# One block for the first batch's product with v, and the steps that stand beside it

## The chip, the cores and the metric

The kernel runs on one core of one Trainium2 chip. The metric is the device time of one execution in microseconds (us); a smaller number is better. The engines are named as in the profile: PE (TensorE), ACT (ScalarE), DVE (VectorE), POOL (GpSimd) and SP (which issues DMAs). A granted clock of 1.00 in the profile is PE's upper level, 2.4 GHz.

## The reference

Two batches of eight heads of attention, with 768 positions of 64 numbers each. A position may look only at positions of its own hash bucket; the bucket is the signs of six projections. The 16 heads' outputs are then the rows of x for a mixture of four experts of two layers each.

```python
q_bits = (np.einsum('bhsd,dk->bhsk', q, proj) > 0)   # 6 bits, the same for k
mask = q_bucket[:, :, :, None] == k_bucket[:, :, None, :]
scores = np.where(mask, scale * np.matmul(q, k.transpose(0, 1, 3, 2)), -1e9)
attn = np.exp(scores - scores.max(-1, keepdims=True)); attn /= attn.sum(-1, keepdims=True) + 1e-09
attn_out = np.matmul(attn, v)                        # batch 2, heads 8, seq 768, head_dim 64
out += p[:, e:e+1] * (np.maximum(x @ w1[e], 0.0) @ w2[e])   # for each of 4 experts
```

## The kernel before

The program has two stages. In the first, the attention of the first batch runs alone, apart from the splitting of the first expert's weights. In the second, the experts' products for the first batch fill PE, and the second batch's attention is woven into them. The edits of this case move work in the first stage only.

`attention()` walks through steps i. Step i is tile t = i mod 6 (128 queries) of head x = i div 6. In each step it calls stages in the order of the letters in `ORDER`, and each engine executes what it was given in the order in which it was given. Each stage works on an older tile or head, by a lag:

- S, scores: four matmuls (L448, L450) into a `sps` tile of PSUM (two tiles in turn), and on DVE a minimum over the row (L455) that also empties `sps`. The second pair of matmuls reads the bucket code in `k2` and `al`.
- E, exponential, lag 1: one ACT instruction (L471).
- T, turning, lag 3: six PE transposes (L516) in two halves, each into a bank of the pool `one` (four banks). A half is emptied by a copy on ACT (L522) or DVE (L520): of three tiles, the first has one copy on each, the second two on ACT, the third one on each. In what follows T0 to T5 are named by the step in which they stand: T3 turns tile 0 of the head, T0 turns tile 3 of the head before.
- V, product with v: twelve column-tiled pairs of matmul records a head (L566) into `pv`, one bank of `one`. `LAG_V` says in which steps after the head's last tile; in the first batch in two parts of six pairs, in steps 3 and 5 of the next head.
- U (L591, L593): `pv` copied out by ACT and DVE, which frees its bank.
- M (L604, L606, L609): three POOL instructions for each half of a pair of heads, in steps 3 and 4 of heads 3, 5 and 7.
- P: the next head's preparation, a generator that goes on by one piece a step. Its pieces are hi (ACT L377 and three POOL copies L265), lo (DVE L380 and one POOL copy), and hash: two pairs of matmuls (L392), their signs by ACT (L402, a pair), and two POOL instructions (L407 and L265) that write the bucket code into `al` and `k2`. The next head's S0 cannot end before that code is there. P also starts the loads of q and k for the head after, and turns them on DVE (L335, here "the turn"), which waits for the hash, since the turned tile takes the place of the one that the hash reads.

Every `W_STEP` pieces of work that `attention()` yields, one piece of the splitting of the first expert's weights is put in (DVE L756, POOL L746).

Of the kernel before, what the change touches and what calls it, by code (L numbers as in the profile page):

```python
# [19 lines left out]
ATT_PACE = 1.52  # L20
LAG_E = 1
SPLIT_AT = (1, 0)
HASH_AT = (3, 0)
LAG_N = (3, 4)
LAG_R = ((6, 4), (7, 6))
LAG_T = 3
LAG_X = 2
LAG_Y = 4
LAG_V = ((4, 6), (7,))
LAST_V = (4, 5)  # L30
LAG_U = (3, 1)
LAG_M = (10, 10)
PP_BUFS = 6
TW = 3
# [9 lines left out]
W_STEP = 6  # L44
PREP_AT = 0
ORDER = "TXSUVMEYNRP"
LIGHT_FROM = 8
DRAIN = 2000
SPLIT_FIRST = 3
FAST = 4  # L50
ALONE = 16
# [5 lines left out]
def tile_lsh_attention__then__domain_moe(  # L57
# [12 lines left out]
    B, H, S, D = q.shape  # L70
    NB = proj.shape[1]
    E, DM, F = w1.shape
    NT = S // P
# [149 lines left out]
    def in_blocks(b, h):  # L223
        return b * H + h in BLOCKS
# [112 lines left out]
    def prep_head(b, h):  # L337
# [27 lines left out]
        else:  # L365
# [4 lines left out]
            steps.setdefault(SPLIT_AT[late] + 1, []).append("lo")  # L370
            steps.setdefault(HASH_AT[late], []).append("hash")
            for at in range(max(steps) + 1):
# [47 lines left out]
    for j in range(KD):  # L420
        t = xp.tile([P, 2, S], F32R, tag=f"x{j}", name="xs0")
# [15 lines left out]
    def mixed(b, h):  # L437
        return b * H + h < LIGHT_FROM

    def heavy(b, h, t):  # L440
        return mixed(b, h)
# [34 lines left out]
    def stage_n(b, h, t):  # L476
        r, o, n = span_of(b, h, t)
        if o != n - 1:
            return
        den = dens.pop((b, h, r))  # L480
        rd = sm.tile([P, NT], F32, tag="rd", name="rd", bufs=2)
        nc.vector.tensor_scalar(out=den[:, :n], in0=den[:, :n], scalar1=1e-9, scalar2=None, op0=ALU.add)
        nc.vector.reciprocal(out=rd[:, :n], in_=den[:, :n])
        rows[b, h, r] = dr.tile([P, n], F32, tag=f"row{n}", name="row", bufs=6)
        nc.sync.dma_start(out=rows[b, h, r], in_=rd[:, :n])

    def stage_r(b, h, t):
        r, o, n = span_of(b, h, t)
        j, odd = divmod(h, 2)
        if t != NT - 1 and (o != n - 1 or not odd):  # L490
            return
        if not odd:
            rdbs[b, j] = xs.tile([P, S], F32, tag="rdb", name="rdb", bufs=1)
        for i in range(r + 1) if not odd else (r,):
            row = rows.pop((b, h, i))
            nc.sync.dma_start(
                out=rdbs[b, j][odd * D : (odd + 1) * D, i * n * P : (i + 1) * n * P],
                in_=row.rearrange("p t -> (p t)").partition_broadcast(D),
            )
# [3 lines left out]
    def stage_t(b, h, t):  # L503
        pt, _ = probs_t.pop((b, h, t))
        g, o = divmod(t, G)
        if o == 0:
            if b or g == 0:
                t0 = pt_tile([P, NT, GN], "pt")
                parts[b, h, g] = [t0[:, a : a + TW] for a in range(0, NT, TW)]
            else:  # L510
                parts[b, h, g] = [hp.tile([P, TW, GN], F32, tag=tag, name="pth") for tag in ("hh", "hl")]
            pts[b, h, g] = [x[:, c] for x in parts[b, h, g] for c in range(TW)]
        for i, a in enumerate(range(0, NT, TW)):
            ps = one("ptps")
            for c in range(TW):
                nc.tensor.transpose(ps[:, c * P : (c + 1) * P], pt[:, (a + c) * P : (a + c + 1) * P], ident)  # L516
            src = ps[:, : TW * P].rearrange("p (c n) -> p c n", c=TW)
            dst = parts[b, h, g][i][:, :, o * P : (o + 1) * P]
            if i and o % 2 == 0:
                nc.vector.tensor_copy(dst, src)  # L520
            else:
                nc.scalar.activation(dst, src, ACTF.Copy)  # L522
# [24 lines left out]
    def stage_y(b, h, g):  # L547
        scr = scrs.pop((b, h, g))
        pt = pt_tile([P, NT, GN], "pt")
        px = pt.rearrange("p c n -> p (c n)")  # L550
        nc.sync.dma_start(out=px.rearrange("p (q x) -> p q x", q=QD), in_=scr.rearrange("q p x -> p q x"))
        px = px.rearrange("p (a c q) -> p c a q", c=NT, q=32)
        pts[b, h, g] = [px[:, c] for c in range(NT)]
# [61 lines left out]
    hseq = [(b, h) for b in range(B) for h in range(H)]  # L615
# [4 lines left out]
    def v_lags(b, h):  # L620
        return LAST_V if (b, h) == (0, H - 1) else LAG_V[not mixed(b, h)]

    def u_lag(b, h):
        return v_lags(b, h)[-1] + (1 if (b, h) == (0, H - 1) else LAG_U[not mixed(b, h)])

# [3 lines left out]
    def attention():  # L629
        n = len(seq)  # L630
        prep = [iter(())]

        def do(op, i):
            if op == "N":
                for b in range(B):
                    j = i - LAG_N[b]
                    if 0 <= j < n and seq[j][0] == b:
                        stage_n(*seq[j])
            elif op == "R":
                for b in range(B):  # L640
                    for odd in range(2):
                        j = i - LAG_R[b][odd]
                        if 0 <= j < n and (seq[j][0], seq[j][1] % 2) == (b, odd):
                            stage_r(*seq[j])
            elif op == "T":
                j = i - LAG_T
                if 0 <= j < n and heavy(*seq[j]):
                    stage_t(*seq[j])
                    return 654
            elif op == "X":  # L650
                j = i - LAG_X
                if 0 <= j < n and not heavy(*seq[j]):
                    stage_x(*seq[j])
            elif op == "Y":
                j = i - LAG_Y
                if 0 <= j < n and j % G == G - 1 and not heavy(*seq[j]):
                    b, h, t = seq[j]
                    stage_y(b, h, t // G)
            elif op == "S":
                if i < n:  # L660
                    b, h, t = seq[i]
                    if t == 0:
                        x = hseq.index((b, h))
                        prep[0] = prep_head(*hseq[x + 1]) if x + 1 < len(hseq) else iter(())
                    stage_s(b, h, t)
                    return 652 + 4270 // NT
                return DRAIN
            elif op == "V":
                for bh, lag in ended(i):
                    for part, at in enumerate(v_lags(*bh)):  # L670
                        if lag == at:
                            stage_v(*bh, part, len(v_lags(*bh)))
                            if (bh, part) == ((0, H - 1), len(v_lags(*bh)) - 1):
                                ready[0] = True
                                return 0
            elif op == "U":
                for bh, lag in ended(i):
                    if lag == u_lag(*bh):
                        stage_u(*bh)
            elif op == "M":  # L680
                for (b, h), lag in ended(i):
                    for g in range(NT // G):
                        if h % 2 and lag == (u_lag(b, h) if (b, h) == (0, H - 1) else LAG_M[b] + g):
                            stage_m(b, h, g)
                if done_b[0] and ready[0]:
                    ready[0] = False
                    return 0
            elif op == "E":
                j = i - LAG_E
                if 0 <= j < n:  # L690
                    stage_e(*seq[j])
            elif op == "P":
                if i < n:
                    b, h, t = seq[i]
                    x = hseq.index((b, h))
                    c = next(prep[0], None) if t >= PREP_AT and x < ALONE else None
                    if t == NT - 1 and x + 2 < len(hseq) and in_blocks(*hseq[x + 2]) and x < ALONE:
                        turn_blocks(*hseq[x + 2])
                    if t == QK_AT and x + 2 < len(hseq):
                        load_qk(*hseq[x + 2])  # L700
                    if t == V_AT and x:
                        load_v(*hseq[x])
                    return c
            return None

        for i in range(n + LAG_M[1] + 3):
            for op in ORDER:
                c = do(op, i)
                if c is not None:
                    yield c  # L710
            x, t = divmod(i, NT)
            if t == NT - 1 and ALONE <= x < len(hseq) - 1:
                for c in prep[0]:
                    yield c
                if x + 2 < len(hseq):
                    turn_blocks(*hseq[x + 2])
                yield ALONE_GAP
# [430 lines left out]
    with tc.manual_schedule():  # L1148
# [6 lines left out]
        i = 0  # L1155
# [21 lines left out]
        for b in range(B):  # L1177
            dm = da = 0.0
            for c in moe(b):
                dm += c  # L1180
                while da < dm * ATT_PACE * n_att / n_moe:
                    x = next(att, None)
# [34 lines left out]
```

## Time and profile before

| | |
|---|---|
| time, median of 3 runs | 706.07 us (705.58 to 706.62) |
| the profiled execution's own time | 705.74 us |
| its span, first to last instruction | 704.0 us |
| PE busy, share of the span | 99% |
| DVE, ACT, POOL busy | 73%, 47%, 44% |
| granted clock of PE | 1.00 throughout |

The profiled execution took 1.7 us more than its span, and it lies 0.33 us under the median of the three runs. A share of busy time is a mean over both stages. PE's matmuls overlap in the profile, so that its busy share hides short waits; the distance from one start to the next tells more.

### The profile page before, as it was taken

The page shows a single profiled execution, that of the slowest core. Times are in us where ns is not written, and L with a number is a line of the kernel's source. Part 1 is how long each engine was busy: PE and PEld are TensorE (multiplying, and loading weights), DVE is VectorE, ACT ScalarE, POOL GpSimd, SP SyncE. Part 2 cuts the span into 40 slices and gives each one's busy share as a digit, 9 for nine tenths or more (in the row PEclk, how much of TensorE's full clock was granted, in tenths as well). Part 3 has the DMA queues.
Part 4 walks back from the last instruction along what each step waited for, and adds up shares of the span by engine and source line. Part 5 has one row for each costly group of instructions (what it writes and reads, how often), then busy time and mean ns, then how long its engine had stood idle before and what let it go on. Part 6 is the DMA issues. An engine that isn't in the chain of part 4 may idle for free.

```text
span 704.0 us, 10120 instructions
## 1 busy us (share of the span) xinstructions
PE 695.8 (99%) x3702; PEld 589.8 (84%) x3702; DVE 513.7 (73%) x840; ACT 330.1 (47%) x645; POOL 307.2 (44%) x290
## 2 busy tenths in 40 slices
PE   8999999999999999999999999999999999999998
PEld 6766676878878878878998989899898989989896
DVE  6898888967668568774767886776767667776862
ACT  6887788544543553551424444243333424343330
POOL 6359578623443543461525555342324324232420
PEclk9999999999999999999999999999999999999999
DMA  5323344759879878683111212421122121122202
GB/s 139 64 52 76 87 104 80 232 168 302 246 223 285 236 251 301 212 284 139 60 63 59 89 63 77 150 71 61 61 89 88 45 78 61 61 60 90 82 9 89
DMA packets 83938, 87.77 MB, mean 125 GB/s; under 512 B 52400, under 2 KB 54960, under 8 KB 81840
## 3 DMA queue, kind: packets, MB, share of 16 engines
q1 hardware_dynamic: 82864, 86.79, 41.1%
q8 instruction: 29, 0.48, 0.3%
q10 hardware_dynamic: 1024, 0.33, 0.2%
q14 instruction: 21, 0.17, 0.1%
HBM read 65.04 MB, written 22.07 MB: 124 GB/s over the span
## 4 chain that ended last, share of the span: by engine, by line
PE 92%; DVE 3%; issue 2%; POOL 2%; ACT 1%; DMA 0%; ACTq 0%; POOLq 0%; DVEq 0%
PE mps L787 12%; PE mps L789 12%; PE mps L788 12%; PE mps L1070 8%; PE mps L1074 8%; PE mps L1073 8%; PE pv L566 8%; PE sps L448 4%; PE sps L450 4%; PE ptps L516 4%; PE mps L837 3%; PE mps L839 3%; PE mps L838 3%; PE hps L392 1%; DVE p L455 1%
## 5 line engine op out<-in xcount | busy, mean ns | idle before, releaser
L787 PE MATMUL mps<-w2hi,hh 128*128 128x512 f32 (+1 forms) x388 | 150.6, 388 | 0.0
L789 PE MATMUL mps<-w2hi,hl 128*128 128x512 f32 (+1 forms) x388 | 150.3, 387 | 0.0
L788 PE MATMUL mps<-w2lo,hh 128*128 128x512 f32 (+1 forms) x388 | 150.3, 387 | 0.0
L1056 POOL TENSOR_TENSOR w2lo<-ws,w2hi 128x512 fp32r<-128x512 f32 x48 | 61.2, 1297 | 150.6 <-ACT w2hi L1055 149.1
L455 DVE TENSOR_SCALAR_CACHE_REDUCE p<-sps 128x768 f32<-128x768 f32 x96 | 90.3, 941 | 26.5 <-PE sps L450 24.9
L471 ACT ACTIVATE p<-p,nb 128x768 f32<-128x768 f32 x96 | 89.5, 932 | 25.3 <-DVE p L455 24.9
L781 DVE SCALAR_TENSOR_TENSOR acc<-mps,pe,acc 128x512 f32<-128x512 f32 (+1 forms) x85 | 63.0, 742 | 49.5 <-PE mps L789 48.8
L1074 PE MATMUL mps<-xo,w1lo 128*128 128x384 f32 x272 | 91.4, 336 | 0.0
L1070 PE MATMUL mps<-xo,w1hi 128*128 128x384 f32 x272 | 91.3, 336 | 0.0
L1073 PE MATMUL mps<-xo,w1hi 128*128 128x384 f32 x272 | 91.3, 336 | 0.0
L1080 ACT ACTIVATE hh<-mps 128x384 fp32r<-128x384 f32 x96 | 47.3, 493 | 92.5 <-PE mps L1074 62.9
L789 PEld LDWEIGHTS mps<-w2hi,hl 128*128 128x128 f32 x388 | 72.9, 188 | 15.3
L787 PEld LDWEIGHTS mps<-w2hi,hh 128*128 128x128 f32 x388 | 72.9, 188 | 14.5 <-issue 0.6
L788 PEld LDWEIGHTS mps<-w2lo,hh 128*128 128x128 f32 x388 | 72.9, 188 | 14.0
L1100 DVE TENSOR_TENSOR mt<-mps,mt 128x384 f32<-128x384 f32 x72 | 40.2, 558 | 44.5 <-PE mps L1074 43.7
L1014 POOL TENSOR_TENSOR w1lo<-ws,w1hi 128x512 fp32r<-128x512 f32 x36 | 49.4, 1377 | 43.8 <-ACT w1hi L1010 16.5
L566 PE MATMUL pv<-pt,tv 128*64 128x384 f32 x288 | 67.2, 492 | 0.0
L1085 DVE SCALAR_TENSOR_TENSOR hl<-mps,hh 128x384 fp32r<-128x384 f32 x96 | 53.4, 556 | 15.4 <-ACT hh L1080 13.1
L1010 ACT ACTIVATE w1hi<-wc 128x512 fp32r<-128x512 f32 x48 | 30.0, 630 | 69.8 <-DVE wc L1019 69.8
L265 POOL TENSOR_SCALAR q<-ah 64x768 fp32r<-64x768 f32 (+1 forms) x33 | 27.1, 823 | 77.3 <-ACT ah L377 63.0
L448 PE MATMUL sps<-ah,q 128*128 128x384 f32 x192 | 54.1, 363 | 1.3 <-DVE p L455 1.3
L535 DVE STREAM_TRANSPOSE t<-p 128x768 f32<-128x768 f32 x48 | 46.2, 963 | 9.3 <-ACT p L471 9.1
(136 smaller groups left out, 1368.8 us busy)
## 6 DMA issues: line engine op xcount, KB each, us to landing
ws<-in_moe_w_dram SPq DMA_DIRECT2D x64, 512.0 KB, 3.7
scr<-t SPq DMA_DIRECT2D x16, 1152.0 KB, 7.9
pt<-scr SPq DMA_DIRECT2D x16, 1152.0 KB, 6.7
tv<-in_v_dram SPq DMA_DIRECT2D x16, 192.0 KB, 4.8
tqk<-in_q_dram SPq DMA_DIRECT2D x30, 96.0 KB, 3.2
out_dram<-acc SPq DMA_DIRECT2D x11, 256.0 KB, 2.0
tqk<-in_k_dram SPq DMA_DIRECT2D x28, 96.0 KB, 3.1
rdb<-row SPq DMA_DIRECT2D x14, 192.0 KB, 4.6
```

The lines of the kernel that those rows point to most:

```text
L448: nc.tensor.matmul(ps[:, i, :NH], q1[:, sl], k1[:, i * NH : (i + 1) * NH], start=True, stop=False)
L455: nc.vector.tensor_scalar(out=two(pt), in0=ps[:, :, :NH], scalar1=MASKED, scalar2=MASKED, op0=ALU.min, op1=ALU.min, accum_out=nb,)
L471: nc.scalar.activation(pt, pt, ACTF.Exp, bias=nb, scale=-1.0, accum_out=dens[b, h, r][:, o : o + 1])
L566: nc.tensor.matmul(dst, vvs[b, h][:, c], pts[b, h, g][c], start=c == 0, stop=c == NT - 1, tile_position=(0, g * D),)
L781: nc.vector.scalar_tensor_tensor(out=acc, in0=ps, scalar=pcol, in1=acc, op0=ALU.mult, op1=ALU.add)
L787: nc.tensor.matmul(ps, hh[:, ts], w2hi[:, f, cs], start=n == 0, stop=False)
L788: nc.tensor.matmul(ps, hh[:, ts], w2lo[:, f, cs], start=False, stop=False)
L789: nc.tensor.matmul(ps, hl[:, ts], w2hi[:, f, cs], start=False, stop=n == FC - 1)
L1056: nc.gpsimd.tensor_tensor(out=lo[:, c + o], in0=t[:, o], in1=hi[:, c + o].bitcast(F32), op=ALU.subtract)
L1070: nc.tensor.matmul(ps, whi[:, kk, fs], xh[kk], start=first and kk == 0, stop=False, skip_group_check=True)
L1073: nc.tensor.matmul(ps, whi[:, kk, fs], xl[kk], start=False, stop=False, skip_group_check=True)
L1074: nc.tensor.matmul(ps, wlo[:, kk, fs], xh[kk], start=False, stop=kk == KH - 1, skip_group_check=True)
```

## The change

For heads 1 to 7, the calls of steps 4 and 5 get orders of their own (`V_ORDERS`). V is one block of twelve pairs in step 4, behind the scores of steps 3 and 4 (S3 and S4), without a T between them. The hash moves from step 3 to step 4, right behind V, and T4 behind the hash. U moves from step 2 of the head after the next to its step 0. The turn moves from step 5 to step 4, for heads 1 to 5. Since the preparation now yields five times a head in place of four, the pieces of the weight splitting also fall elsewhere. No instruction is added or removed.

```diff
-HASH_AT = (3, 0)
+HASH_AT = (4, 0)
...
-LAG_V = ((4, 6), (7,))
+LAG_V = ((5,), (7,))
 LAST_V = (4, 5)
-LAG_U = (3, 1)
+LAG_U = (2, 1)
...
 ORDER = "TXSUVMEYNRP"
+V_ORDERS = {4: "XSEVPTUMYNR", 5: "SXTUVMEYNRP"}
...
-                    if t == NT - 1 and x + 2 < len(hseq) and in_blocks(*hseq[x + 2]) and x < ALONE:
+                    if t == (4 if 0 < x < H - 2 else NT - 1) and x + 2 < len(hseq) and in_blocks(*hseq[x + 2]) and x < ALONE:
                         turn_blocks(*hseq[x + 2])
...
         for i in range(n + LAG_M[1] + 3):
-            for op in ORDER:
+            x, t = divmod(i, NT)
+            for op in V_ORDERS.get(t, ORDER) if 0 < x < H else ORDER:
                 c = do(op, i)
                 if c is not None:
                     yield c
-            x, t = divmod(i, NT)
```

On PE, before, from the hash in head 2 to the second half of V (`hps` is the hash, `ptps` T, `sps` S, `pv` V):

```order
L392 MATMUL hps<-xt,pf 44x384 x2
L516 MATMUL ptps<-ident,p 128x128 x6
L448 MATMUL sps<-ah,q_374 128x384 x2
L450 MATMUL sps<-k_377,al 128x384 x2
L516 MATMUL ptps<-ident,p 128x128 x6
L448 MATMUL sps<-ah,q_374 128x384 x2
L450 MATMUL sps<-k_377,al 128x384 x2
L566 MATMUL pv<-pt,tv 64x384
```

And in the changed kernel from a hash on, one head later, up to the next head's S0 and T1:

```order
L393 MATMUL hps<-xt,pf 44x384 x2
L517 MATMUL ptps<-ident,p 128x128 x6
L449 MATMUL sps<-ah,q_540 128x384 x2
L451 MATMUL sps<-k_543,al 128x384 x2
L517 MATMUL ptps<-ident,p 128x128 x12
L449 MATMUL sps<-ah,q_714 128x384 x2
L451 MATMUL sps<-k_717,al 128x384 x2
L517 MATMUL ptps<-ident,p 128x128 x6
```

Between the hash and the next head's S0 there were T4, S4, T5, S5, six pairs of V and T0; now there are T4, S5, T5 and T0.

On ACT, before, from the signs of head 3 to the next hi (`k` is written by the signs, `pt` and `pth` by T's copies, `p` by E):

```order
L402 ACTIVATE k_715<-hps,sgn_bias 44x384 x2
L522 ACTIVATE pt<-ptps 128x3x128 x2
L471 ACTIVATE p,den<-p,nb 128x768
L522 ACTIVATE pt<-ptps 128x3x128
L471 ACTIVATE p,den<-p,nb 128x768
L522 ACTIVATE pth<-ptps 128x3x128
L471 ACTIVATE p,den<-p,nb 128x768
L522 ACTIVATE pth<-ptps 128x3x128 x2
L471 ACTIVATE p,den<-p,nb 128x768
L377 ACTIVATE ah<-xt,qk_scale 128x768
```

And in the changed kernel, the same place:

```order
L403 ACTIVATE k_717<-hps,sgn_bias 44x384 x2
L523 ACTIVATE pt<-ptps 128x3x128 x3
L472 ACTIVATE p,den<-p,nb 128x768
L523 ACTIVATE pth<-ptps 128x3x128
L594 ACTIVATE xr<-pv 64x384
L472 ACTIVATE p,den<-p,nb 128x768
L523 ACTIVATE pth<-ptps 128x3x128 x2
L472 ACTIVATE p,den<-p,nb 128x768
L378 ACTIVATE ah<-xt,qk_scale 128x768
```

The exponential of tile 3 went ahead of the signs, and U's copy (`xr`) came in between the signs and the exponential of the next head's tile 0 (the last `p` row).

On POOL, before, from the hi copies of head 3 to its bucket code (the last two rows):

```order
L265 TENSOR_SCALAR q_712<-ah 64x768 x2
L265 TENSOR_SCALAR k_715<-ah 64x768
L746 TENSOR_TENSOR w1lo<-ws,w1hi 128x512
L265 TENSOR_SCALAR ah<-al 64x768
L604 TENSOR_TENSOR xr<-xr,rdb 128x384
L606 TENSOR_SCALAR xs_114<-xr 128x384
L609 TENSOR_TENSOR xs_114<-xr,xs_114 128x384
L407 TENSOR_SCALAR al<-k_715,bit_mul 44x768
L265 TENSOR_SCALAR k_715<-al 12x768
```

And in the changed kernel:

```order
L266 TENSOR_SCALAR q_714<-ah 64x768 x2
L266 TENSOR_SCALAR k_717<-ah 64x768
L747 TENSOR_TENSOR w1lo<-ws,w1hi 128x512
L266 TENSOR_SCALAR ah<-al 64x768
L605 TENSOR_TENSOR xr<-xr,rdb 128x384
L607 TENSOR_SCALAR xs_114<-xr 128x384
L610 TENSOR_TENSOR xs_114<-xr,xs_114 128x384
L747 TENSOR_TENSOR w1lo<-ws,w1hi 128x512
L408 TENSOR_SCALAR al<-k_717,bit_mul 44x768
L266 TENSOR_SCALAR k_717<-al 12x768
```

A second piece of the weight splitting (`w1lo`) now stands ahead of the bucket code in head 3. In head 5 one such piece (`w2lo`) came in behind the hi copies, where there was none.

## Rows read from the trace of the kernel before

**Rows 1.** Window, length, busy us of PE, PEld, DVE, ACT, POOL; clock, DMA share, GB/s.

```profile
22.12:120.91 98.79, 97.97 (x625) 67.16 (x625) 84.75 (x164) 81.97 (x172) 67.72 (x72) 1.00 0.38 77
```

**Rows 2.** Timeline of PE in head 4: start, length, engine, line, what.

```profile
62.12 0.82 PE L516 MATMUL ptps<-ident,p 128*128 128x128 f32 x6
62.69 0.59 PE L448 MATMUL sps<-ah,q 128*128 128x384 f32 x2
...
63.48 0.96 PE L516 MATMUL ptps<-ident,p 128*128 128x128 f32 x6
...
65.07 0.54 PE L566 MATMUL pv<-pt,tv 128*64 128x384 f32 x1
...
65.44 0.49 PE L566 MATMUL pv<-pt,tv 128*64 128x384 f32 x1
...
67.05 0.81 PE L392 MATMUL hps<-xt,pf 128*44 128x384 f32 x4
67.80 0.87 PE L516 MATMUL ptps<-ident,p 128*128 128x128 f32 x6
...
70.90 0.54 PE L566 MATMUL pv<-pt,tv 128*64 128x384 f32 x1
...
72.98 0.87 PE L516 MATMUL ptps<-ident,p 128*128 128x128 f32 x6
```

**Rows 3.** Timeline of PE: head 1's T3, T4; head 7's T4; head 8.

```profile
22.12 0.87 PE L516 MATMUL ptps<-ident,p 128*128 128x128 f32 x6
...
26.35 0.87 PE L516 MATMUL ptps<-ident,p 128*128 128x128 f32 x6
...
109.25 0.90 PE L516 MATMUL ptps<-ident,p 128*128 128x128 f32 x6
...
120.11 0.52 PE L448 MATMUL sps<-ah,q 128*128 128x384 f32 x2
...
120.91 0.54 PE L566 MATMUL pv<-pt,tv 128*64 128x384 f32 x1
```

**Rows 4.** Timeline of ACT, and one wait of PE for it in head 0.

```profile
67.97 1.17 ACT L402 ACTIVATE k<-hps,sgn_bias 44x384 fp32r<-44x384 f32 x2 [1.12 <-PE hps L392]
69.17 0.87 ACT L522 ACTIVATE pt<-ptps 128x384 f32<-128x384 f32 x2
...
74.92 0.87 ACT L522 ACTIVATE pth<-ptps 128x384 f32<-128x384 f32 x2
75.68 0.94 ACT L471 ACTIVATE p<-p,nb 128x768 f32<-128x768 f32 x1
...
76.60 0.93 ACT L377 ACTIVATE ah<-xt,qk_scale 128x768 fp32r<-128x768 f32 x1
...
16.78 0.94 ACT L471 ACTIVATE p<-p,nb 128x768 f32<-128x768 f32 x1
...
17.86 0.87 PE L516 MATMUL ptps<-ident,p 128*128 128x128 f32 x6 [0.61 <-ACT p L471]
```

**Rows 5.** Timeline of POOL in head 3, a copy of head 5, and PE's wait.

```profile
49.73 1.79 POOL L265 TENSOR_SCALAR q<-ah 64x768 fp32r<-64x768 f32 x2 [4.81 <-ACT ah L377]
...
52.51 1.85 POOL L746 TENSOR_TENSOR w1lo<-ws,w1hi 128x512 fp32r<-128x512 f32 x1
...
55.36 1.22 POOL L604 TENSOR_TENSOR xr<-xr,rdb 128x384 f32<-128x384 f32 x1
...
58.43 0.91 POOL L407 TENSOR_SCALAR al<-k,bit_mul 44x768 fp32r<-44x768 f32 x1
59.42 0.83 POOL L265 TENSOR_SCALAR k<-al 12x768 fp32r<-12x768 f32 x1
60.33 1.27 POOL L746 TENSOR_TENSOR w1lo<-ws,w1hi 128x512 fp32r<-128x512 f32 x1
...
77.61 1.71 POOL L265 TENSOR_SCALAR q<-ah 64x768 fp32r<-64x768 f32 x2 [5.99 <-PE ptps L516]
...
60.30 0.62 PE L450 MATMUL sps<-k,al 76*128 76x384 f32 x2 [0.35 <-POOL k L265]
```

## The prediction

> **What bounds the kernel now.** I read the page first: PE is busy for 99% of the span, at a granted clock of 1.00. Then the busy times of the stretch in which the change lies, from T3 of head 1, the last thing that both kernels have alike, to the V of head 7 that stands in head 8: 98.79 us [rows 1]. PE is busy 97.97 of them, DVE 84.75, ACT 81.97, POOL 67.72. So PE sets the pace there, but two engines are at 83 to 86%, and any longer wait for them shows at once. The timeline of PE gives the pieces of a head, from start to start [rows 2]: T to S 0.57, S to T 0.79, half a V to the hash 1.98, of which the last five pairs take 1.61 (0.32 each), hash to T4 0.75. From T4 of head 1 to T4 of head 7 are 82.90 us, 13.82 a head [rows 3].
>
> Behind that stretch the order of every engine is what it was, and PE goes on to be busy, so I count what is won or lost there as it is on the whole time.
>
> **What PE itself saves.** The second V block cost 2.08 to T0 [rows 2], and six more pairs in one block cost 6 x 0.32 = 1.93: 0.15 less, the way in and out. The way from S into V is 0.80 [rows 3], that from S to T 0.79, so there is no more to it: 0.16 us a head, 1.1 for seven heads. The Trainium skill, TensorEngine Tiling (Array Packing), section Key Properties, says that a change of the tiling mode drains TensorE; V is column-tiled and S and T aren't, so the trace agrees with it, at 0.16 us a block, and by that rule alone the time would be 1.1 us less.
>
> Without any wait a head would be, from T4 to the next T3: four times T to S, 2.28, four times S to T, 3.16, and T5 to T0 without an S between, 0.65 (my estimate between 0.57 and the 0.82 that six transposes last), 6.09 in all; then T3 to S3 0.57, S3 to S4 0.79, S4 to V 0.80, V 1.98 + 1.93 = 3.91, hash to T4 0.75: 6.82. Sum 12.91, against 13.82 now; the difference is more than the drain, since 13.82 has waits in it.
>
> **What the new order makes late: ACT.** This is the step on which I decide. The signs of the hash wait for the hash, and start 0.17 behind T4's start, as now (67.80, 67.97). Before them ACT has run out of work, since for 6 us (S3, S4, V, hash) PE gives it nothing to copy. From them on its queue is, in the program's order: signs 1.20 (67.97 to 69.17), three copies of T4 and T5 at 0.38 (the pair at 74.92 took 0.76), exponential of tile 4 0.92 (75.68 to 76.60), T0's copy 0.38, U 0.38, exponential of tile 5 0.92, T1's two copies 0.76, and only then the exponential of the next head's tile 0 [rows 4]. That begins 0.17 + 1.20 + 1.14 + 0.92 + 0.38 + 0.38 + 0.92 + 0.76 = 5.87 behind T4's start. T3 transposes that tile, and a T that waits for an exponential starts 1.08 behind its start (16.78, 17.86). So T3 starts at 6.95, where PE alone would be at 6.09. The inputs come earlier than ACT's turn for them: T0 needs the bank of T4's second half, whose copy ends at 0.17 + 1.20 + 0.38 + 0.49 = 2.24, so T0 starts at 2.3 and S0 at 2.9, 3 us ahead of the exponential of its tile, with one DVE instruction between. So the queue has no gaps to shrink. Before the change six pairs of V lay between T5 and T0, in which ACT caught up; that cover is gone. The skill's TensorE: Matmul & The Clock Gate, section on the array's architecture, says that ACT and DVE are strict first-in-first-out queues; the order of the trace agrees, and by it nothing lets tile 0's exponential pass the others.
>
> A head is then 6.95 + 6.82 = 13.77, which is 13.82 over again. PE's gain turns into a wait of T3 (and, ahead of it, of T5, T0 and T2, for banks and exponentials). The chain is exact to about 0.15 a head: a copy is 0.49 long (a pair 0.87), and U or a pair costs 0.11 more where what follows waits for its end.
>
> **POOL.** The bucket code must be in `k2` before the second pair of S0's matmuls. From the hash to there PE had about 6.2 us of other work (T4 at 67.80 to T0 at 72.98, and 1.0 more); now it has 2.9 to S0 (0.3 of it T5's and T0's wait for banks) and half of S0's 0.79, 3.3. The signs end at 1.37, and the two POOL instructions take 0.99 and 0.83 [rows 5]: 3.2. It just fits, if POOL is free. In head 3 it isn't: hi starts behind the exponential of tile 0, at 5.87 + 0.92 = 6.79, its first POOL copy 1.01 later (76.60, 77.61) at 7.80; then three copies 2.78, w1lo and the low part's copy 2.85, M 3.07, and the second w1lo 1.27: the bucket code starts at 17.77, that is 4.0 behind the next T4, and S0's second pair at 4.0 + 0.99 + 0.83 + 0.05 = 5.9 (5.3 if the first w1lo takes 1.27 and not 1.85). From there to T3 it is 3.18 (60.30 to 63.48), so T3 is at 9.1 (8.5) in place of 6.95: 1.5 to 2.1 lost, I take 1.8. In head 5, with one w2lo and M, it is 1.27 earlier: 0.2 to 0.8 lost, I take 0.4. In head 7, without a piece of weights, 7.80 + 2.78 + 0.92 + 3.07 = 14.6 is ahead of the signs' end (15.1): nothing; likewise the even heads, whose M stands behind the code. Sum 2.2. Before, the same lateness in head 3 cost 0.35, since it had the longer cover.
>
> **What costs nothing.** The turn (0.97 on DVE) now runs right behind the hash, where DVE waits for S5's scores, which stand behind T4; if that cover were gone it would push the copies of T5 and T0 by 0.97, which the wait of T3 (0.86) would nearly hide. It frees the slot for the loads of q and k earlier, and the loads on SP keep most of a head to land; v's load stays a head ahead of its V. U frees its bank two steps earlier, which can only shorten T's waits. S4 directly behind S3 needs the `sps` tile of S2, whose scores ended a T and an S before; DVE's one minimum in between covers it, and if it were late the wait would be a part of that one instruction, below 0.9.
>
> **Sum.** From 22.12: T3 to T4 of head 1 6.82; six heads at 13.77 82.62; POOL 2.2; from T4 of head 7 to the V in head 8 the same ACT queue, with hi 0.93 and a second pair of signs 1.20 ahead of T1's copies, one exponential and the copy that V reads (0.49 and 0.05): 9.46. Together 101.1, against 98.79: 2.3 us more. The profiled execution's 705.74 becomes 708.0; the median of the runs shown is 0.33 above that execution, so 708.4 is what I expect of a median.
>
> **Rivals.** (1) ACT's queue doesn't bind, and PE goes at its own pace: faster. By 12.91 a head, and 7.65 at the end (T4 to V in head 8 by the same pieces), the stretch would be 6.82 + 77.46 + 7.65 = 91.9; with 0.3 a head for the banks of T5 and T0, 94.0: 4.8 us less, 701.3. For it: PE at 97.97 of 98.79 us, and ACT at 83%. Against it: the 5.87 above. It decides from the point where tile 0's exponential starts 0.4 earlier than 5.87, which gives back the 2.3. (2) ACT binds as said, but POOL's lateness doesn't reach S0 (weights split elsewhere, or shorter M): 0.1 more (the sum without the 2.2), no change, 706.2. For it: in head 5 the margin is a few tenths; against: in head 3 it needs 1.9 us. (3) The chain is longer, by the slower case named for U and for one pair of copies: 0.22 for seven heads, 1.5 on top, 709.9. For it: the pair at 69.17 may have been such a case; against: the one at 74.92 wasn't.
>
> **How the numbers follow.** About 0.2% (1.4 us) is what a measurement of this kernel can tell from no change. Forecast 0.50, rival 1 0.17, rival 2 0.20, rival 3 0.13. So faster 0.17, same 0.20, slower 0.63. The range leaves out rival 1 and little else: its low end is 704.0, a chain 0.5 a head shorter with POOL as reckoned at its least; its high end 711.0, rival 3 with POOL's upper bound (2.9). The likeliest case alone spans 707 to 710.
>
> **What the changed profile would show.** Right: twelve V pairs in one row, 3.9 long; T4 to T4 13.8 in heads without M; ACT without idle time from the signs to tile 0's exponential, and idle for over 1.5 us ahead of the signs; PE's T3 waiting for ACT's exponential; S0's second pair in head 4 waiting some 2 us for POOL's `k2`, in head 6 under 1 us. Wrong: T3 starting 6.1 to 6.4 behind T4 (then rival 1), or no wait for POOL (rival 2). What would make me wrong above all is an ACT queue that starts earlier than the hash's end lets it, or that is shorter than its rows say.

## The result, and the profile after

The changed kernel takes 712.96 us (median of 4 runs, 711.74 to 713.18) beside 705.83 for the kernel before on the same chip: a ratio of 1.0098, 95% interval 1.0085 to 1.0111. It is slower, as forecast, but by 7.1 us and not by 2.3. The profiled execution took 713.05, its span is 711.3 (704.0 before). Three of the four executions, the profiled one among them, have a mean granted clock of 0.997 to 0.998 and took 712.88 to 713.18; the fourth has 1.000 and took 711.74.

First the same stretch as in [rows 1], from T3 of head 1 to the V of head 7 in head 8 (window, length, busy us of PE, PEld, DVE, ACT, POOL; clock, DMA share, GB/s):

```profile
22.10:127.72 105.62, 100.42 (x626) 68.98 (x625) 85.28 (x164) 82.00 (x172) 68.58 (x72) 0.98 0.35 72
```

The busy times of DVE, ACT and POOL are the same to within 1 us; the stretch is 6.83 longer (98.79 before, 101.1 predicted), so nearly all of the loss lies here. PE's busy time itself has grown by 2.45, and the clock's mean is 0.98: part of the stretch ran at a lower clock. Which heads lost it, PE's timeline tells (T3 and T4 of head 1, T4 of heads 2 to 7, then V in head 8), to be read beside [rows 3]:

```profile
22.10 0.87 PE L517 MATMUL ptps<-ident,p 128*128 128x128 f32 x6
...
28.98 0.87 PE L517 MATMUL ptps<-ident,p 128*128 128x128 f32 x6
...
42.86 0.87 PE L517 MATMUL ptps<-ident,p 128*128 128x128 f32 x6
...
57.09 0.88 PE L517 MATMUL ptps<-ident,p 128*128 128x128 f32 x6
...
74.45 0.88 PE L517 MATMUL ptps<-ident,p 128*128 128x128 f32 x6
...
88.67 0.87 PE L517 MATMUL ptps<-ident,p 128*128 128x128 f32 x6
...
103.97 0.87 PE L517 MATMUL ptps<-ident,p 128*128 128x128 f32 x6
...
118.41 0.88 PE L517 MATMUL ptps<-ident,p 128*128 128x128 f32 x6
...
127.72 0.86 PE L567 MATMUL pv<-pt,tv 128*64 128x384 f32 x2
```

From T4 to T4 it is 13.88, 14.23, 17.36, 14.22, 15.30 and 14.44, 89.43 together, where 84.82 was predicted. The two ends come out close to the reckoning: 6.88 ahead of T4 of head 1 (6.82), 9.31 behind T4 of head 7 (9.46). So the miss of 4.6 is in these six distances. From here on, "in head x" means from T4 of head x to T4 of the next head. Head 3's 17.36 (from 57.09) is the largest; PE's timeline from S0 of the next head to its T3:

```profile
60.07 0.60 PE L449 MATMUL sps<-ah,q 128*128 128x384 f32 x2
62.83 0.62 PE L451 MATMUL sps<-k,al 76*128 76x384 f32 x2 [2.17 <-POOL k L266]
63.29 1.19 PE L517 MATMUL ptps<-ident,p 128*128 128x128 f32 x6
64.13 0.99 PE L449 MATMUL sps<-ah,q 128*128 128x384 f32 x2
...
65.56 1.48 PE L517 MATMUL ptps<-ident,p 128*128 128x128 f32 x6
...
67.62 0.60 PE L517 MATMUL ptps<-ident,p 128*128 128x128 f32 x4
```

The wait for the bucket code is there, at 5.74 behind T4 (reckoned: 5.3 to 5.9). But behind it the same instructions are slower: six transposes last 1.48 where they last 0.82 to 0.96 in the rows of before. The window from S0's second pair to T3 says why:

```profile
62.83:67.62 4.79, 4.79 (x22) 4.63 (x23) 3.04 (x6) 3.60 (x7) 4.59 (x5) 0.64 0.31 112
```

The mean clock is 0.64: for 3.4 us from 63.6 the granted clock was at its lower level, 1.2 GHz. The way from the wait to T3 took 4.79 in place of the 3.18 that I took from before: 1.61 more, of which nothing stands in the prediction.

ACT's queue in head 4 (T4 at 74.45), beside [rows 4]:

```profile
74.63 1.16 ACT L403 ACTIVATE k<-hps,sgn_bias 44x384 fp32r<-44x384 f32 x2 [1.76 <-PE hps L393]
75.82 1.26 ACT L523 ACTIVATE pt<-ptps 128x384 f32<-128x384 f32 x3
77.11 0.94 ACT L472 ACTIVATE p<-p,nb 128x768 f32<-128x768 f32 x1
...
78.04 0.47 ACT L523 ACTIVATE pth<-ptps 128x384 f32<-128x384 f32 x1
78.53 0.48 ACT L594 ACTIVATE xr<-pv 64x384 f32<-64x384 f32 x1
79.05 0.94 ACT L472 ACTIVATE p<-p,nb 128x768 f32<-128x768 f32 x1
...
79.98 0.85 ACT L523 ACTIVATE pth<-ptps 128x384 f32<-128x384 f32 x2
80.72 0.93 ACT L472 ACTIVATE p<-p,nb 128x768 f32<-128x768 f32 x1
```

The order is the predicted one, with ACT idle for 1.76 ahead of the signs and never behind them. Tile 0's exponential starts at 6.27 behind T4, not 5.87. T3 is at 81.80, 1.08 behind it as reckoned: 7.35, not 6.95.

```profile
81.80 0.77 PE L517 MATMUL ptps<-ident,p 128*128 128x128 f32 x5
```

The 0.40 are three steps: the three copies take 1.29 and not 1.14, T0's copy 0.49 and U 0.52 and not 0.38 each, all from start to start; at each of these places one instruction ran at its full length before the next began. In head 1, T0's copy and U take 0.37 each; what makes the difference I haven't found.

The other waits of PE in this stretch, apart from two of 0.30 of T for an exponential, are 1.00 for the bucket code in head 5 (at 93.25), 0.36 at 98.41 for DVE (S4 behind S3, waiting for the minimum that empties `sps`), and, in head 8's own steps, one that the prediction had not named at all, 0.70 for the turn:

```profile
98.41 0.61 PE L449 MATMUL sps<-ah,q 128*128 128x384 f32 x2 [0.36 <-DVE p L456]
...
123.12 0.85 PE L393 MATMUL hps<-xt,pf 128*44 128x384 f32 x4 [0.70 <-DVE xt L336]
```

### The profile page after: what moved, and what is told of

Its sections match the earlier page's. It is cut to its first block, busy times and chain, and to the rows that moved or that the text cites. A ratio compares the mean times of both kernels' runs of the same rounds, so it can differ in the third digit from the quotient of the medians.

```text
span 711.3 us, 10126 instructions
## 1 busy us (share of the span) xinstructions
PE 698.6 (98%) x3702; PEld 592.0 (83%) x3702; DVE 514.2 (72%) x840; ACT 330.5 (46%) x645; POOL 308.9 (43%) x290
## 4 chain that ended last, share of the span: by engine, by line
PE 89%; POOL 3%; issue 3%; DVE 2%; ACT 2%; DMA 0%; POOLq 0%; DVEq 0%; ACTq 0%
PE mps L788 12%; PE mps L790 12%; PE mps L789 12%; PE mps L1071 8%; PE mps L1075 8%; PE mps L1074 8%; PE pv L567 8%; PE sps L449 3%; PE sps L451 3%; PE mps L838 3%; PE mps L840 3%; PE mps L839 3%; PE ptps L517 2%; PE hps L393 1%; DVE p L456 1%
```

## The experiments

Below, "T3 behind T4" is the distance from T4's start to the start of the next head's T3, in which ACT's queue shows (7.35 in head 4 of the changed kernel). Each ratio is to the kernel before, run on the same chip, with its 95% interval.

**The hash back in step 3, the rest changed** (between S3 and S4, ahead of V).

```diff
-HASH_AT = (4, 0)
+HASH_AT = (3, 0)
```

> The changed kernel (713.0 us) with the hash alone put back to step 3, ahead of S4 and V; V stays one block. My theory says that the loss lies in what stands behind the hash: the signs of ACT go ahead of V again, and POOL's bucket code gets 6 us of cover. Then T4 to T4 falls from 14.2 to about 13.5 us, no PE wait for POOL is left, the granted clock is 1.00 throughout, and the time is 703 to 705. Rival: the block of V, with two sets of scores ahead of it and no T between them, is itself what costs (ACT and DVE starve during V); then the time stays at 710 or above.

709.43, ratio 1.0047 (1.0035 to 1.006), a miss. The profiled execution is its slowest, 710.42, with 3.4 us at the lower clock near 12 us, ahead of the stretch. PE still waits 0.85 for POOL in head 3, and 1.49 for the turn in head 7. With the signs gone from behind T4, T3 behind T4 falls only to about 7.0 in even heads and 6.73 in head 1, a third of a microsecond for 1.2 us of work taken out. So the signs aren't the whole of the term. In head 4 (T4 at 73.22) ACT now has gaps:

```profile
73.81 0.87 ACT L523 ACTIVATE pt<-ptps 128x384 f32<-128x384 f32 x2 [1.43 <-PE ptps L517]
75.16 0.49 ACT L523 ACTIVATE pt<-ptps 128x384 f32<-128x384 f32 x1 [0.48 <-PE ptps L517]
75.55 0.93 ACT L472 ACTIVATE p<-p,nb 128x768 f32<-128x768 f32 x1
```

Tile 4's exponential (75.55) stands behind the first copy of T5 in the program. Its input, the minimum of S4, is there over 3 us earlier (DVE ends it at 72.13), while V runs and ACT idles (the 1.43 ahead of 73.81).

**The weight pieces where they were** (the fifth yield of the preparation isn't counted).

```diff
-                    yield 654 if at == 1 else 0
+                    yield 654 if at == 1 else 0 if at < 4 else None
```

> The changed kernel with the preparation's fifth yield not counted, so that the pieces of the weight splitting stand where they stood before: in head 3 the second w1lo goes behind the bucket code (in head 5 a w2lo stays ahead of it). If POOL's queue is what S0 waits for in head 4, the wait of 2.17 us there falls to about 0.9, the clock does not drop behind it, and the time falls by 1.3 for the wait and 1 to 1.5 for the clock, to about 710.3. If the wait comes from the hash's late signs and not from POOL's queue, nothing changes (713).

710.39, ratio 1.0059 (1.0045 to 1.0072), as expected: 2.6 of the 7.1 come back. In head 3 the wait of S0's second pair is 0.97 and not 2.17, the clock stays at 1.00 there, and T3 behind T4 is 7.71 and not 10.53. The window behind the wait:

```profile
61.80:65.00 3.20, 3.20 (x24) 3.09 (x25) 2.57 (x6) 3.02 (x7) 3.03 (x4) 1.00 0.00 0
```

**M one step later** (behind the bucket code).

```diff
-LAG_M = (10, 10)
+LAG_M = (11, 10)
```

> The changed kernel with M one step later in the first batch, so that its three POOL instructions stand behind the bucket code in heads 3, 5 and 7. By my theory no wait of PE for POOL is left, head 3 falls from 17.4 to 14.2 and head 5 from 15.3 to 14.2, the clock stays at 1.00, and ACT's queue alone remains: 708.5 to 709. If POOL were the whole loss, the time would be 706 or below.

710.04, ratio 1.0054 (1.004 to 1.0068). Less than expected: in the profiled execution heads 3 and 5 have no wait for POOL now, and the clock stays at 1.00, but head 6's code comes late instead, since the second half of M and a weight piece push that head's hi copies:

```profile
104.52 0.61 PE L451 MATMUL sps<-k,al 76*128 76x384 f32 x2 [1.33 <-POOL k L266]
```

**Copies from ACT to DVE** (the second copies of T4 and T1).

```diff
-            if i and o % 2 == 0:
+            if i:
                 nc.vector.tensor_copy(dst, src)
```

> The changed kernel with the second copy of T4 and T1 on DVE in place of ACT: two copies (0.76 us) less between the signs and the exponential of tile 0, for DVE which waits there. If ACT's queue binds, T4 to T4 falls by 0.7 in all heads (hi and with it POOL's work also come 0.7 earlier), 4 to 5 us in all, to 708.5. If PE's own order or POOL binds, the time changes by less than 1 us, or rises, since DVE is as busy as ACT.

713.66, ratio 1.0107 (1.0092 to 1.0123): nothing gained, a miss. Nine waits of PE now end with DVE's minimum (3 in the changed kernel), and two T wait for a bank:

```profile
PE sps L449 <- DVE p L456: 3.6, 9, 1.0
PE ptps L517 <- ACT pth L523: 1.8, 2, 0.9
PE sps L451 <- POOL k L266: 1.6, 1, 1.6
```

So DVE, with 85 us in the stretch, has no room for these copies. I went on to the order of ACT's work.

**Tile 4's exponential ahead of the signs** (a letter `e`, which issues it in step 4 right behind tile 3's).

```diff
-V_ORDERS = {4: "XSEVPTUMYNR", 5: "SXTUVMEYNRP"}
+V_ORDERS = {4: "XSEeVPTUMYNR", 5: "SXTUVMYNRP"}
```

> The changed kernel (713.0 us) with one more edit: the exponential of tile 4 is issued in step 4, right behind that of tile 3 and ahead of V, the signs and the copies of T4 and T5 (before it stood behind T5's first copy, though its scores S4 now come ahead of V). Theory after the first runs: ACT idles during V and then has too long a queue up to tile 0's exponential. If so, that queue is 0.92 shorter, T4 to T4 falls from 14.2 to about 13.4 in heads 2, 4, 6 and 7, the POOL waits of heads 3 and 5 stay, and the time is about 709. Rival: PE waits for DVE or for banks just as long (as in the run that moved copies to DVE); then 712 or more.

710.87, ratio 1.0065 (1.0052 to 1.0079): 2 us better than the changed kernel, less than expected. T3 behind T4 is 6.50 and 6.65 in heads 1 and 4, but 7.40 in heads 2 and 5, where the minima of S3 and S4 are late on DVE, the two exponentials end behind the hash, and push the signs.

**The same with M later and the weight pieces back.** The three edits together, each as its diff stands above.

> The exponential of tile 4 ahead as in the other run, and POOL relieved by both means: M one step later and the pieces of the weight splitting where they were before. Both of the losses that I name (ACT's queue, POOL's lateness with the clock behind it) are then gone: T4 to T4 about 13.4 in all heads, no wait for POOL, clock 1.00, 704 to 705.5, that is, a little faster than before. If something else in the new order costs (the block itself), it stays above 708.

709.79, ratio 1.005 (1.0036 to 1.0064), some 5 us over what was expected. DVE is now late in head 5, where the weight pieces and M run beside it. DVE, POOL, ACT and PE there:

```profile
93.94 1.15 DVE L759 CAST w2hi<-ws 128x512 fp32r<-128x512 f32 x1
95.02 1.23 DVE L483 TENSOR_SCALAR den<-den 128x6 f32<-128x6 f32 x1
...
96.39 1.43 DVE L381 SCALAR_TENSOR_TENSOR al<-xt,qk_scale,ah 128x768 fp32r<-128x768 f32 x1
```

```profile
93.81 1.00 POOL L610 TENSOR_TENSOR xs<-xr,xs 128x384 fp32r<-128x384 f32 x1
94.78 1.45 POOL L749 TENSOR_TENSOR w2lo<-ws,w2hi 128x512 fp32r<-128x512 f32 x1
```

```profile
99.26 0.94 ACT L472 ACTIVATE p<-p,nb 128x768 f32<-128x768 f32 x1 [3.80 <-DVE p L456]
...
100.20 0.92 ACT L472 ACTIVATE p<-p,nb 128x768 f32<-128x768 f32 x1
...
101.23 1.16 ACT L403 ACTIVATE k<-hps,sgn_bias 44x384 fp32r<-44x384 f32 x2
102.42 0.87 ACT L523 ACTIVATE pt<-ptps 128x384 f32<-128x384 f32 x2
```

```profile
102.45 0.84 PE L517 MATMUL ptps<-ident,p 128*128 128x128 f32 x4 [1.23 <-ACT k L403]
```

The minimum of S3 is late, so tile 3's exponential is late (ACT idles for 3.80 ahead of it). So the signs start at 101.23, behind both exponentials, though the hash ended near 99.7, and T5 waits 1.23 for a bank. With the signs behind V, one late minimum passes through the whole chain.

**The signs ahead too.** The exponential ahead, and the hash in step 3:

```diff
-HASH_AT = (4, 0)
+HASH_AT = (3, 0)
...
-V_ORDERS = {4: "XSEVPTUMYNR", 5: "SXTUVMEYNRP"}
+V_ORDERS = {4: "XSEeVPTUMYNR", 5: "SXTUVMYNRP"}
```

> The exponential of tile 4 ahead, and the hash in step 3 (its signs then go ahead of the exponentials of tiles 3 and 4, all under the cover of V). ACT's queue from T4 to tile 0's exponential then has neither signs nor tile 4's exponential: T4 to T4 13.3 to 13.5 (the hash as a block of its own costs PE 0.2), POOL's wait in head 3 as it was with the hash in step 3 (0.85), 704 to 706. If ACT isn't what binds, it stays at the 709.4 that the hash in step 3 alone gave.

707.54, ratio 1.0022 (1.0013 to 1.0031). T3 behind T4 is 6.30 in odd and 6.37 in even heads, apart from heads 3 and 6. Either edit alone left ACT's queue binding in most heads; the two together free it. What is left is POOL's 0.88 in head 3, a T3 some 0.7 later in head 6 (7.01), and the wait for the turn:

```profile
117.91 0.85 PE L393 MATMUL hps<-xt,pf 128*44 128x384 f32 x4 [1.52 <-DVE xt L336]
```

**The plain order of steps** (T4, S4, V, hash, T5, S5, T0, S0).

```diff
-V_ORDERS = {4: "XSEVPTUMYNR", 5: "SXTUVMEYNRP"}
+V_ORDERS = {}
```

> The changed kernel without its own orders for steps 4 and 5: V is still one block in step 4 with the hash behind it, but T4 stands ahead of S4 and V, so ACT has T4's copies during V, and only one set of scores stands ahead of it. By the theory of ACT's queue behind V (0.78 shorter, since T4's two copies go ahead of the signs) T4 to T4 falls to 13.5 in heads without M, and the time to about 709 with POOL's waits as they were. If the two sets of scores ahead of V are a gain, as the change has it, the time rises above 713.

724.15, ratio 1.0253 (1.0239 to 1.0267), a miss by 15 us. From the hash to S0 PE has 2.96 us here (3.73 in the changed kernel), so every head from 1 to 7 waits for the bucket code, for 0.6 to 0.85 in the first two and for 4.34 and 4.45 in heads 3 and 5. Each of the two long waits has 6.8 us at the lower clock from 64.9 and 99.0 on:

```profile
66.78 1.01 PE L451 MATMUL sps<-k,al 76*128 76x384 f32 x2 [4.34 <-POOL k L266]
```

The window behind it:

```profile
66.50:74.00 7.50, 7.22 (x36) 6.96 (x37) 4.57 (x9) 4.97 (x10) 3.92 (x5) 0.65 0.42 85
```

So the change's orders, with T4 behind the hash, are a gain over the plain one.

**The turns of heads 6 and 7 in step 4 as well** (on top of the kernel of 707.54).

```diff
-                    if t == (4 if 0 < x < H - 2 else NT - 1) and x + 2 < len(hseq) and in_blocks(*hseq[x + 2]) and x < ALONE:
+                    if t == (4 if 0 < x < H else NT - 1) and x + 2 < len(hseq) and in_blocks(*hseq[x + 2]) and x < ALONE:
```

> The kernel with the hash in step 3 and the exponential of tile 4 ahead of the signs took 707.54; its largest wait was 1.52 us, of the hash at 117.91 for the turn that stands in step 5 of head 7, behind the minimum of S5, which in the changed order comes behind the whole block of V. Here that turn stands in step 4 of heads 6 and 7 too. Theory (the rest of the loss is that wait and POOL's 0.88 in head 3): 706.0, as fast as the kernel before. Rival (PE has nothing ready behind that hash anyway): 707.5.

706.91, ratio 1.0007 (0.9998 to 1.0016), between the two. The wait of 1.52 is gone; S0 to S0 from head 8 to head 9 falls by 1.07, the median by 0.63; where the rest went I haven't followed.

**And M later on top of that.**

```diff
-LAG_M = (10, 10)
+LAG_M = (11, 10)
```

> The same with M one step later, behind the bucket code in heads 3, 5 and 7 (LAG_M 11). Theory (POOL's lateness in head 3, 0.88, and what DVE's and POOL's code lose behind M in head 6, some 0.6, are the last that is not PE's own): 704.5 to 705.2. Rival (M pushes the hi copies of the even heads, as it did when it was moved alone, and the code of heads 4 or 6 is late by some 1 us): 706 to 707.

705.26, ratio 0.9985 (0.9976 to 0.9994): faster than the kernel before by 0.15%, just above what was expected. In the stretch of [rows 1] the profile lists no wait of PE, and the page's chain of waits (shares of the span) is PE's almost alone (89% in the changed kernel, with 3% POOL and 2% each ACT and DVE):

```profile
PE 97%; DVE 1%; ACT 1%; issue 0%; DMA 0%; ACTq 0%
```

ACT in head 5 (T4 at 84.18, T3 at 90.48, 6.30): both exponentials run during V, and behind T4 ACT waits for PE, no longer PE for ACT.

```profile
81.78 0.94 ACT L472 ACTIVATE p<-p,nb 128x768 f32<-128x768 f32 x1 [0.26 <-DVE p L456]
...
83.08 0.93 ACT L472 ACTIVATE p<-p,nb 128x768 f32<-128x768 f32 x1 [0.27 <-DVE p L456]
...
84.76 0.87 ACT L523 ACTIVATE pt<-ptps 128x384 f32<-128x384 f32 x2 [0.65 <-PE ptps L517]
86.12 0.49 ACT L523 ACTIVATE pt<-ptps 128x384 f32<-128x384 f32 x1 [0.49 <-PE ptps L517]
...
89.20 0.93 ACT L472 ACTIVATE p<-p,nb 128x768 f32<-128x768 f32 x1
```

The stretch takes 96.92 (22.97 to 119.89), 1.87 less than before. Of that gain 1.18 are lost ahead of it in this execution: from the first T to T3 of head 1 it takes 11.39, against 10.21 before, since 3.4 us there run at the lower clock:

```profile
10.60:16.00 5.40, 5.32 (x24) 4.86 (x25) 4.19 (x9) 3.68 (x8) 1.87 (x3) 0.68 0.56 190
```

**The last kernel without the exponential ahead.**

```diff
-V_ORDERS = {4: "XSEeVPTUMYNR", 5: "SXTUVMYNRP"}
+V_ORDERS = {4: "XSEVPTUMYNR", 5: "SXTUVMEYNRP"}
```

> The kernel that took 705.26 (hash in step 3, exponential of tile 4 ahead of T4's copies, turns of heads 6 and 7 in step 4, M later), with the exponential of tile 4 back behind T5's first copy. Theory (ACT keeps its program order, so that this exponential, whose input is ready about 3 us earlier, sits behind T5's copy and pushes tile 0's): tile 0's exponential at 5.65 to 5.95 behind T4's start in place of 5.02 to 5.30, T3 at 6.7 to 7.0 in place of 6.3, some 0.5 a head more in six or seven heads: 708.3 to 709. Rival (with the signs in step 3 ACT has room enough, and PE sets the pace): 705.3.

708.11, ratio 1.0036 (1.0023 to 1.0048). T3 behind T4 is 6.73 in odd and 7.00 in even heads, as expected; the exponential's place alone is worth some 3 us here. ACT in head 5 (T4 at 85.87), where tile 4's exponential stands behind T5's copy again, as in the first experiment:

```profile
88.20 0.93 ACT L472 ACTIVATE p<-p,nb 128x768 f32<-128x768 f32 x1
```

**M later in the kernel before.** The same line as above, `LAG_M = (11, 10)`, and nothing else of the change.

> The kernel before with M one step later alone, to see whether the gain of the 705.26 kernel over the kernel before is the block of V or only M's place. Theory (the block, with ACT's order mended, gives the gain; POOL's lateness cost the kernel before 0.35 in head 3 alone): 705.6 to 706.1. Rival (M's place is what gains): 705.3 or less.

706.34, ratio 1.0006 (0.9997 to 1.0015): no change. So the gain of the 705.26 kernel isn't M's place alone. Whether the block of V is what gains isn't shown: no run has the kernel before with its exponentials or turns moved and V in two parts.

## Why the prediction was wrong

The sign and the two causes were right, the size wasn't: 712.96, outside the range to 711.0. The 4.61 by which T4 of head 1 to T4 of head 7 is longer than predicted divide so, from the trace:

- **POOL in head 3, sized without the clock: 1.8 more than predicted.** The code's lateness was right: S0's second pair at 5.74 behind T4, and 3.18 more would have made T3 8.92, 1.97 lost where I took 1.8. T3 was at 10.53; the other 1.61 are the lower clock behind the wait. The step that failed is "from there to T3 it is 3.18", which held the clock at the 1.00 of the trace before. The kernel with the pieces back, whose wait is 0.97, keeps its clock: with the pieces go the long wait and the slow clock behind it. That the wait of 2.17 is what lowers the clock is likely but not shown: in the trace the clock falls 0.8 us behind the wait's end, and one of the four executions, at 711.74, kept its clock. So this part of the loss, 1.1 to 1.4 us by those times, isn't in every execution; without it the time is still outside the range.
- **ACT, tile 0's exponential at "5.87 behind T4's start": 1.2 more.** The mechanism was right, the size wasn't: it is 6.27 in even heads, which puts T3 0.39 later three times, and 0.06 later in head 1. That ACT's queue binds is shown by the kernels of 707.54 and 708.11, which differ from their neighbours in ACT's order. My claim that the chain is exact to 0.15 was wrong: steps at full length are 0.40 in one head. It is rival 3, which I gave 0.13, with 0.39 in place of 0.22. The gaps that I read from before (0.38 a copy) came from places where the next instruction began before the copy's end (74.92 and 0.87 long, the next at 75.68).
- **POOL in head 5: 0.4 more.** S0's second pair at 4.58, T3 at 7.75: 0.80 lost, the upper end of the 0.2 to 0.8 given, and not 0.4.
- **S4 directly behind S3, which stands under "What costs nothing": 1.2**, from T3 to T4: 0.73 ahead of T4 of head 6, 0.28 ahead of T4 of head 7, 0.19 in the four others together. Behind the late S0 of head 6, DVE is late with the minimum of S2, and S4 waits (98.41). I had bounded it by 0.9 and taken nothing. This part is read from the trace of the changed kernel; no run took it out alone.

**The turn.** Where it was moved, no wait of PE for it is listed. For heads 6 and 7 it was left in step 5, and there S5, whose minimum stands ahead of it on DVE, now comes behind the whole block of V: 0.70 at 123.12, which I didn't see. It is inside the 9.31 that matched the 9.46, so something else in that piece was shorter by as much; I haven't followed what.

**PE's saving.** Ahead of T4 of head 1, V starts at 24.31 and the hash at 28.23: 3.92 for the block, as reckoned. That it doesn't show in the time is ACT's queue and POOL's lateness: in the kernel of 705.26, T4 to T4 is 13.44 to 13.57 in heads 1 to 5 and 13.83 in head 6, a mean of 13.57 against 13.82 before.

**Rivals 1 and 2** fell. Rival 1 was to decide from an exponential 0.4 earlier than 5.87; the kernel of 705.26 has it at 5.02 to 5.30 in heads 1 to 5, and gains 0.9, not the 4.8 reckoned. T3 behind T4 is then 6.3, as rival 1 had it; but T3 to T4 takes 7.14 to 7.26, not 6.82, with the hash between S3 and S4, and from T4 of head 1 to T4 of head 6 it is 67.58, only 1.49 under the 69.07 of before. Rival 2 had no wait for POOL; there were two.

## What to carry to other kernels

A block that lets PE run alone takes away its cover twice: the engines that feed it run out of work during the block, and then have everything to do at once behind it. Look, before such a move, for work whose input is ready during the block but that stands in its engine's program behind something that waits for the block's end; here one exponential and the pair of signs, and both had to move. And price a wait of PE with what comes behind it: here 1.61 us at a slower clock behind a wait of 2.17, and 0.73 more, with a late minimum, behind one of 1.00.

## What of the hardware was not expected

PE's granted clock fell to 1.2 GHz behind a wait of 2.17 us, for 3.4 us, and around each of two waits of 4.34 and 4.45, for 6.8 us. It did not in profiles whose longest waits there were 1.33, 1.52 and 1.58. But waits aren't all of it: in the kernel of 705.26, and in the profiled execution with the hash back in step 3, the lower level stood for 3.4 us near 12 us, where the longest wait of PE nearby is 0.36. The other profiles, that of the changed kernel among them, have the same wait there and keep the clock. Of whole executions, a mean clock of 0.998 or less is found in all four of the kernel with the waits of 4.34 and 4.45, in three of four of the changed kernel, in 5 of 60 of the kernel before, and in 5 of 11 of the kernel of 705.26, which has no long wait. So a long wait isn't needed for it, and what brings it in a given execution isn't settled.

An instruction of DVE on 6 elements a partition (`den`, 95.02) took 1.23, and 0.17 at 79.13 in the kernel of 707.54; it ends as POOL's `w2lo` ends (94.78 to 96.23), and the cast ahead of it (93.94 to 95.09) likewise runs on past the end of POOL's row before that (94.81). The Trainium skill, SBUF — State Buffer, section Who interferes with whom, says that DVE in some modes and POOL share one pair of ports, and that whichever starts second is held until the first has ended. The traces agree: in the kernel of 705.26, seven of the ten rows of `den` up to 140 us, 0.33 to 0.85 long, end 0.02 to 0.04 behind the end of a row of POOL; the other three stand inside a merged row of two POOL copies. No kernel here varied it. By that rule POOL's work lengthens DVE's instructions, and a profile counts this as DVE's busy time.
